# The diagonal tile of inverse softmax sums with its row blocks innermost, and a new order of issue

## The chip, the core and the metric

The kernel runs on one core of a Trainium2 chip. The core has five engines that run side by side, each through its own queue of instructions in order: TensorE (PE in the profile; matmuls, and PEld for the loading of their stationary operand), VectorE (DVE), ScalarE (ACT), GpSimd (POOL) and SyncE (SP), which here only issues transfers to the 16 DMA engines. SBUF is the working memory of 128 partitions, PSUM the memory that TensorE writes. An instruction on one engine that needs a result of another waits for a semaphore; everything behind it on its own queue waits with it. The metric is the time of one execution on the device, in microseconds.

## What is computed

Attention over 4 batches of 12 heads, 448 positions and 64 features, then a gated block with a product over positions, then a layer norm with a feed-forward block of 768 to 3072 to 768 and a residual. Cut to what matters:

```python
def _attn_ref(q, k, v, g_q, g_k):
    q_n, k_n = (rmsnorm(q, g_q), rmsnorm(k, g_k))
    scores = scale * np.matmul(q_n, k_n.transpose(0, 1, 3, 2))
    scores = scores - np.max(scores, axis=-1, keepdims=True)
    attn = np.exp(scores)
    attn = attn / (np.sum(attn, axis=-1, keepdims=True) + 1e-09)
    return np.matmul(attn, v).astype(np.float32)
...
def _moe_ref(x, w_in, w_spatial, b_spatial, w_out):
    h = np.maximum(x @ w_in, 0.0)
    u, v = (h[..., :d_ff // 2], h[..., d_ff // 2:])
    v_n = (v - mu) / np.sqrt(var + 1e-06)
    v_s = np.einsum('ts,bsd->btd', w_spatial, v_n) + b_spatial[None, :, None]
    return ((u * v_s) @ w_out).astype(np.float32)
...
def _moe2_ref(x, g_ln, w_ch1, w_ch2):
    xn = (x - mu) / np.sqrt(var + 1e-06) * g_ln
    ch = np.maximum(xn @ w_ch1, 0.0) @ w_ch2
    return (x + ch).astype(np.float32)
```

## The kernel before

The 48 heads are worked through as 24 pairs (`i` = 0 to 23; six pairs make a batch). A pair occupies the 128 partitions as 2 heads of 64. The 448 positions of a head are cut into 64 x 7: a position is `s = 7 * p + n`, with `p` from 0 to 63 and the row block `n` from 0 to 6 (`NB` = 7). So the queries of row block `n` are positions n, 7 + n, 14 + n and so on.

For each pair, `att_load` brings q, k and v (tiles `raw`, `vraw`); `att_front` and `att_back` normalise q and k (squares `sq`, row sums `ss`, factors `rs`, the product `raw` at L200, a split into two 16-bit halves `qk` at L202 and L203) and transpose them by DMA into `hT` (L206, L208). `s_mm` (L240) makes the scores of one or two row blocks in PSUM (`ps_s`), `softmax1` takes their maxima (`nb`, L251, VectorE) and the exponentials with their sums (`pexp` and `sm`, L256, ScalarE), and `softmax2` transposes the exponentials, on TensorE for the first six pairs (`ps_t`, `pT`) and by DMA for the others (`p`, `pT`). `av_mm` multiplies with v into `ps_o`, which holds the 64 features of both heads on the partitions and the 448 queries along the free dimension, row block by row block: column `64 * n + p`.

The division by the sums comes last. `av_scale` inverts the sums (`sm`, 128 x 7), splits them into two 16-bit parts (`s16`, named `s` in the profile) and multiplies them with a doubled 64 x 64 unit matrix (`eye2`, `eye` in the profile) into a tile `dg` of diagonals (L314, VectorE). Two matmuls with a matrix of ones per head (`head`, L319) spread `dg` over the partitions into `ps_r`; ScalarE copies it to `rb` (L321). `av_out` multiplies `ps_o` with `rb` into `xo` (L332, VectorE), now in the order of the positions, column `7 * p + n`, and splits it into two 16-bit halves `xT`. Both inputs of L332 are read through a rearrangement, `d (n p) -> d p n`, so they step 64 elements from one output element to the next.

Beside the attention of pairs 0 to 6 the weights of the gated block are prepared. Weights come as 64-bit floats, and VectorE makes 32-bit floats of each block in three integer steps (L420 to L422; blocks `v_w`, `u_w`, `o_w`, later `r_w`). The gated block of a batch (`moe1`: `psv`, `psu`, `pss`, `pso`) runs beside the attention of the next batch, that of the last batch beside layer norms and weights of the feed-forward block, which fills the time from 590 us on (`ps1` and `ps`, L729 and L780).

The order of all instructions is set at the end by `issue_order`. It reads the finished program, gives each instruction a cost by rules (`hold`, `LAT`), and lists the engines' work forwards and backwards in turn; the priorities of a pass come from the ends of the one before. A table `SHAKES` of triples (seed, spread, passes) perturbs the priorities at each entry and lists again. The last list becomes the order on every engine, held by dependencies that `add_manual_dep` adds; SP's list, and so the order of the transfers, is one of them. For VectorE the costs depend on sizes, types and memories, not on steps between elements.

Of the kernel before, what the change touches and what calls it, by code (L numbers as in the profile page):

```python
# [10 lines left out]
F16 = mybir.dt.float16  # L11
# [4 lines left out]
ALU = mybir.AluOpType  # L16
# [4 lines left out]
P = 128  # L21
B, H, S, D = 4, 12, 448, 64
NB = 7
# [280 lines left out]
def av_scale(c, i):  # L304

    nc = c.nc
    p = c.pr[i]
    nc.vector.tensor_scalar(p.sm, p.sm, 1e-9, None, op0=ALU.add)
    nc.vector.reciprocal(p.sm, p.sm)
    s16 = c.small.tile([P, 2, NB], F16, tag="s16", name=f"s16_{i}", bufs=2)  # L310
    nc.vector.tensor_scalar(s16[:, 0], p.sm, 2.0 ** 15, None, op0=ALU.mult)
    nc.vector.scalar_tensor_tensor(s16[:, 1], p.sm, 2.0 ** 15, s16[:, 0], op0=ALU.mult, op1=ALU.subtract)
    dg = c.att.tile([P, 2, NB, 64], F16, tag="dg", name=f"dg{i}", bufs=1)
    nc.vector.tensor_tensor(dg.rearrange("p t n q -> p (t n) q"),  # L314
                            s16.rearrange("p t n -> p (t n)").unsqueeze(2).to_broadcast([P, 2 * NB, 64]),
                            c.eye2[:].unsqueeze(1).to_broadcast([P, 2 * NB, 64]), op=ALU.mult)
    pr = c.ps_o.tile([P, 512], F32, tag="ps_o", name=f"ps_r{i}")
    for t in range(2):
        nc.tensor.matmul(pr[:, :S], c.head, dg[:, t].rearrange("p n q -> p (n q)"), start=(t == 0), stop=(t == 1))  # L319
    p.rb = c.att.tile([P, S], F32, tag="rb", name=f"rb{i}", bufs=1)  # L320
    nc.scalar.activation(p.rb, pr[:, :S], AF.Copy, scale=2.0 ** -15 if i in PE_PAIRS else 2.0 ** -29)  # L321


def av_out(c, i):
    nc = c.nc
    p = c.pr[i]
    b, hp = i // NPAIR, i % NPAIR
    if hp == 0:
        c.xT[b] = c.xpools[b % 2].tile([P, NC6, 2, S], F16, tag="xT", name=f"xT{b}")
    xT = c.xT[b]  # L330
    x = c.att.tile([P, S], F32, tag="xo", name=f"xo{i}", bufs=1)
    nc.vector.tensor_tensor(x.rearrange("d (p n) -> d p n", n=NB), p.po[:, :S].rearrange("d (n p) -> d p n", n=NB),  # L332
                            p.rb.rearrange("d (n p) -> d p n", n=NB), op=ALU.mult)
    if i in PE_PAIRS:
        split(c, x, xT[:, hp, 0, :], xT[:, hp, 1, :], c.sv[b][:, 0:1])
    else:
        nc.scalar.activation(xT[:, hp, 0, :], x, AF.Copy)
        nc.vector.tensor_tensor(xT[:, hp, 1, :], x, xT[:, hp, 0, :], op=ALU.subtract)
    del c.pr[i]
# [6 lines left out]
def att_slot(c, i, n):  # L346
# [25 lines left out]
    if i > 0:  # L372
        av_scale(c, i - 1)
        av_mm(c, i - 1)
        yield AV_COST
        av_out(c, i - 1)
# [17 lines left out]
def split(c, raw, hi, lo, scale):  # L394

    c.nc.scalar.activation(hi, raw, AF.Copy, scale=scale)  # L396
    c.nc.vector.scalar_tensor_tensor(lo, raw, scale, hi, op0=ALU.mult, op1=ALU.subtract)
# [399 lines left out]
def weave(a, b):  # L797

    out = [iter(a), iter(b)]
    while out:  # L800
        for g in list(out):
# [10 lines left out]
WINDOW = 3413  # L812


SHAKES = ((0, 0, 2), (556, 3000, 2), (1748, 20000, 1), (1711, 1000, 3), (1453, 8000, 1), (1124, 20000, 1), (257, 300,
# [3 lines left out]


def free_size(ap):
# [225 lines left out]
def issue_order(tc):  # L1047
# [3 lines left out]
    prio = [float(o.n) for o in g.ops]  # L1051
    for seed, spread, passes in SHAKES:
        rnd = random.Random(seed)
# [205 lines left out]
```

## Time and profile before

| what | value |
|---|---|
| median of 3 runs | 1159.89 us (1159.18 to 1160.92) |
| the profiled execution | 1165.11 us on the device |
| its span, first to last instruction | 1163.3 us |
| mean granted clock of TensorE | 0.97 of full speed |
| busy: TensorE, VectorE, ScalarE, GpSimd | 1051.7, 959.1, 587.3, 269.5 us |
| instructions | 16645 |

A busy TensorE means that a matmul is under way, not that it runs at its best rate. Stages are given as stretches of the profiled span, "58:174" from 58 to 174 us. In the rows, names are those of the tiles with their numbers left out, and `a<-b,c` means that a is written from b and c. The DMA share is the mean busy share of the 16 DMA engines; the clock is what TensorE was granted, 1.00 being 2.4 GHz and 0.50 being 1.2 GHz.

### The profile page before, as it was taken

Reading aid. Unit: us, or ns where it says so; the run is one execution under the profiler, and the core shown is the slowest. Engines: PE = TensorE matmul, PEld = TensorE weight load, DVE = VectorE, ACT = ScalarE, POOL = GpSimd, SP = SyncE. Lnnn points to the kernel's source line nnn. Section 1 sums busy time; section 2 is a strip of 40 time slices with the busy share of each in tenths; the row PEclk is TensorE's granted clock in tenths of the full one; section 3 lists DMA queues with packets and bytes.
Section 4 is the critical chain, followed back from the end, with each engine's and each line's share of the span. In section 5 each row is a group of like instructions: output and inputs, shape, how many; then the busy total and the mean of one; then the engine's idle time right before and its main releaser. Section 6 shows DMA issues by size and latency. Waiting matters only on the chain.

```text
span 1163.3 us, 16645 instructions
## 1 busy us (share of the span) xinstructions
PE 1051.7 (90%) x6190; PEld 543.4 (47%) x6190; DVE 959.1 (82%) x1641; ACT 587.3 (50%) x1128; POOL 269.5 (23%) x193
## 2 busy tenths in 40 slices
PE   0689579998889989897699999999999999999998
PEld 0344234444344434443355555555555555555554
DVE  7799999969997996979979788787878878787545
ACT  2899977767776884556532333142432323243110
POOL 3453653418445511222101101010110101011000
PEclk9999879999899999988899999999999999999999
DMA  7997999898999997879572222202121221110004
GB/s 240 233 234 207 189 181 190 160 233 162 205 179 212 182 166 194 183 183 250 127 195 82 82 83 58 78 28 82 34 76 66 74 78 46 65 51 32 1 28 163
DMA packets 249088, 154.46 MB, mean 133 GB/s; under 512 B 209904, under 2 KB 226224, under 8 KB 249008
## 3 DMA queue, kind: packets, MB, share of 16 engines
q1 hardware_dynamic: 244624, 142.40, 51.9%
q10 hardware_dynamic: 4384, 11.01, 3.1%
q8 instruction: 48, 0.79, 0.3%
q14 instruction: 32, 0.26, 0.1%
HBM read 86.40 MB, written 11.01 MB: 84 GB/s over the span
## 4 chain that ended last, share of the span: by engine, by line
PE 45%; DVE 8%; DMA 1%; ACT 1%; issue 1%; POOL 0%; DVEq 0%; ACTq 0%
PE ps L780 24%; PE ps1w L729 6%; PE ps1z L729 6%; PE ps1x L729 6%; PE ps1y L729 3%; DVE x L784 2%; DVE w1v L537 1%; DVE x L694 1%; DMA r_w<-in_moe_w_ch_dram 1%; DVE h L742 1%; DVE lst L681 0%; ACT r_f L525 0%; DVE r_f L422 0%; DVE r_f L421 0%; POOL rsr_x L567 0%
## 5 line engine op out<-in xcount | busy, mean ns | idle before, releaser
L780 PE MATMUL ps<-w,h 128*128 128x384 f16 x2016 | 385.9, 329 | 13.2 <-ACT w L396 5.1
L780 PEld LDWEIGHTS <-h 128*128 128x128 f16 x2016 | 197.2, 98 | 164.4 <-issue 15.1
L784 DVE SCALAR_TENSOR_TENSOR x<-ps,wio,x 128x768 f32<-128x768 f32 x168 | 169.5, 1013 | 75.2 <-PE ps L780 74.3
L729 PEld LDWEIGHTS <-w1v 128*128 128x128 f16 x1512 | 147.0, 98 | 127.4 <-issue 3.7
L240 PE MATMUL ps_s<-hT 128*64 128x448 f16 x672 | 104.4, 392 | 26.1 <-ACT pexp L256 20.3
L256 ACT ACTIVATE pexp<-ps_s,nb 128x448 f32<-128x448 f32 x168 | 106.1, 645 | 25.8 <-DVE nb L251 23.0
L528 POOL TENSOR_TENSOR sums<-r_f 128x384 f32<-128x384 f32 x12 | 12.1, 1011 | 457.7 <-ACT r_f L525 457.7
L729 PE MATMUL ps1x<-xnT,w1v 128*128 128x448 f16 x432 | 108.4, 352 | 0.2 <-DVE tc L736 0.2
L729 PE MATMUL ps1z<-xnT,w1v 128*128 128x448 f16 x432 | 106.3, 352 | 0.0
L729 PE MATMUL ps1w<-xnT,w1v 128*128 128x448 f16 x432 | 105.2, 352 | 1.0 <-DVE tu L736 0.9
L251 DVE TENSOR_REDUCE nb<-ps_s 128x2 f32<-128x896 f32 x96 | 91.8, 964 | 9.4 <-PE ps_s L240 8.9
L240 PEld LDWEIGHTS <-hT 128*64 128x64 f16 x672 | 39.6, 116 | 80.4 <-issue 53.1
L276 DVE SCALAR_TENSOR_TENSOR p<-pexp,p 128x896 f16<-128x896 f32 x72 | 72.7, 1014 | 4.6 <-ACT p L275 4.1
L185 POOL TENSOR_TENSOR rs<-ss,mhalf 128x28 f32<-128x28 f32 (+1 forms) x12 | 60.0, 4997 | 29.1 <-DVE ss L182 20.9
L203 POOL TENSOR_TENSOR qk<-raw,qk 128x896 f16<-128x896 f32 x23 | 46.1, 2005 | 78.7 <-ACT qk L202 67.5
L613 PE MATMUL psu<-xT,w_u 128*128 128x448 f16 x288 | 61.9, 357 | 2.1 <-ACT vr L595 2.0
L591 PE MATMUL psv<-w_v,xT 128*128 128x512 f16 (+1 forms) x360 | 63.5, 339 | 0.1
L275 ACT ACTIVATE p<-pexp 128x896 f16<-128x896 f32 x72 | 61.3, 857 | 2.6 <-DMA pT<-p 2.4
L741 ACT ACTIVATE h<-td 128x448 f16<-128x448 f32 x24 | 13.8, 574 | 93.1 <-DVE td L736 93.1
L650 PE MATMUL pso<-w_o,g 128*128 128x384 f16 x288 | 52.9, 327 | 1.9 <-ACT g L636 1.1
L631 PE MATMUL pss<-w_sp,vn 128*128 128x448 f16 (+1 forms) x176 | 46.7, 381 | 8.8 <-DVE u L635 7.4
L729 PE MATMUL ps1y<-xnT,w1v 128*128 128x448 f16 x216 | 53.0, 352 | 0.9 <-DMA xnT<-x 0.9
(229 smaller groups left out, 1672.3 us busy)
## 6 DMA issues: line engine op xcount, KB each, us to landing
r_w<-in_moe_w_ch_dram SPq DMA_DIRECT2D x48, 768.0 KB, 4.4
raw<-in_q_dram SPq DMA_DIRECT2D x24, 224.0 KB, 3.7
raw<-in_k_dram SPq DMA_DIRECT2D x24, 224.0 KB, 4.4
vpre<-in_v_dram SPq DMA_DIRECT2D x12, 448.0 KB, 4.8
hT<-hT SPq DMA_DIRECT2D x48, 112.0 KB, 3.1
vraw<-in_v_dram SPq DMA_DIRECT2D x24, 224.0 KB, 3.7
lv<-x2d SPq DMA_DIRECT2D x16, 336.0 KB, 4.5
x<-x2d ACTq DMA_DIRECT2D x14, 384.0 KB, 4.2
```

The source lines that it names most:

```text
L185: nc.gpsimd.tensor_tensor(rs, ss, c.mhalf[:, 0:14 * m], op=ALU.pow)
L240: nc.tensor.matmul(ps[hd * 64:hd * 64 + 64, :S], p.hT[:, blk, hd * 64:hd * 64 + 64], kt[:, :, hd * 64:hd * 64 + 64], start=(t == 0), stop= ...
L251: nc.vector.tensor_reduce(nb[:, 0:n], ps[:, 0:n, :S], axis=AX.X, op=ALU.max, negate=True)
L256: nc.scalar.activation(pe[:, j, :], ps[:, j, :S], AF.Exp, bias=nb[:, j:j + 1], scale=1.0, accum_out=p.sm[:, blk:blk + 1])
L275: nc.scalar.activation(p16[:, 0:n, 0], x, AF.Copy, scale=2.0 ** 14)
L276: nc.vector.scalar_tensor_tensor(p16[:, 0:n, 1], x, 2.0 ** 14, p16[:, 0:n, 0], op0=ALU.mult, op1=ALU.subtract)
L591: nc.tensor.matmul(ps[m * h:m * h + m, 0:hn], xT[:, k, x, t * P:t * P + m], wv[:, w, k, h * hn:(h + 1) * hn], start=(n == 0), stop=(n == l ...
L613: nc.tensor.matmul(ps[:, :S], wu[:, w, k, f * P:(f + 1) * P], xT[:, k, x, :], start=(n == 0), stop=(n == len(mms) - 1))
L650: nc.tensor.matmul(ps[:, 0:384], g16[:, f, g, s0:s0 + m], wo[:, w, f, e * 384:(e + 1) * 384], start=(n == 0), stop=(n == len(mms) - 1))
L729: nc.tensor.matmul(ps, w[:, a, x, d], xnT[:, :, 21 * y + 3 * b + d], start=first and n == 0, stop=n == 8, skip_group_check=True)
L780: nc.tensor.matmul(ps[:, e, 0:QK], h16[:, f, x, t * P:(t + 1) * P], w2[:, y, f, e * QK:(e + 1) * QK], start=n == 0, stop=n == 5)
L784: nc.vector.scalar_tensor_tensor(x2, ps[:, :, 0:QK], io[:, 0:1], x2, op0=ALU.mult, op1=ALU.add)
```

## The change

In `av_scale`, `dg` is laid out as `[P, 2, 64, NB]` instead of `[P, 2, NB, 64]`: of its 896 elements per partition the 7 row blocks are now next to each other. Its two inputs are broadcast accordingly, `s16` over the 64 in the middle and `eye2` over the 7 innermost; before, `s16` was broadcast over the innermost 64. The output of L314 is contiguous before and after. `ps_r` and `rb` then stand in the order of the positions, and `av_out` reads `rb` contiguously; `ps_o` is still read with a step of 64. Sizes, types and the number of instructions are the same.

The second part is the table `SHAKES`, 14 entries in place of 23, of which a line each is shown:

```diff
@@ -310,13 +310,12 @@
     s16 = c.small.tile([P, 2, NB], F16, tag="s16", name=f"s16_{i}", bufs=2)
     nc.vector.tensor_scalar(s16[:, 0], p.sm, 2.0 ** 15, None, op0=ALU.mult)
     nc.vector.scalar_tensor_tensor(s16[:, 1], p.sm, 2.0 ** 15, s16[:, 0], op0=ALU.mult, op1=ALU.subtract)
-    dg = c.att.tile([P, 2, NB, 64], F16, tag="dg", name=f"dg{i}", bufs=1)
-    nc.vector.tensor_tensor(dg.rearrange("p t n q -> p (t n) q"),
-                            s16.rearrange("p t n -> p (t n)").unsqueeze(2).to_broadcast([P, 2 * NB, 64]),
-                            c.eye2[:].unsqueeze(1).to_broadcast([P, 2 * NB, 64]), op=ALU.mult)
+    dg = c.att.tile([P, 2, 64, NB], F16, tag="dg", name=f"dg{i}", bufs=1)
+    nc.vector.tensor_tensor(dg, s16[:].unsqueeze(2).to_broadcast([P, 2, 64, NB]),
+                            c.eye2[:].unsqueeze(1).unsqueeze(3).to_broadcast([P, 2, 64, NB]), op=ALU.mult)
     pr = c.ps_o.tile([P, 512], F32, tag="ps_o", name=f"ps_r{i}")
     for t in range(2):
-        nc.tensor.matmul(pr[:, :S], c.head, dg[:, t].rearrange("p n q -> p (n q)"), start=(t == 0), stop=(t == 1))
+        nc.tensor.matmul(pr[:, :S], c.head, dg[:, t].rearrange("p q n -> p (q n)"), start=(t == 0), stop=(t == 1))
     p.rb = c.att.tile([P, S], F32, tag="rb", name=f"rb{i}", bufs=1)
     nc.scalar.activation(p.rb, pr[:, :S], AF.Copy, scale=2.0 ** -15 if i in PE_PAIRS else 2.0 ** -29)
 
@@ -330,7 +329,7 @@
     xT = c.xT[b]
     x = c.att.tile([P, S], F32, tag="xo", name=f"xo{i}", bufs=1)
     nc.vector.tensor_tensor(x.rearrange("d (p n) -> d p n", n=NB), p.po[:, :S].rearrange("d (n p) -> d p n", n=NB),
-                            p.rb.rearrange("d (n p) -> d p n", n=NB), op=ALU.mult)
+                            p.rb.rearrange("d (p n) -> d p n", n=NB), op=ALU.mult)
     if i in PE_PAIRS:
         split(c, x, xT[:, hp, 0, :], xT[:, hp, 1, :], c.sv[b][:, 0:1])
     else:
...
-SHAKES = ((0, 0, 2), (556, 3000, 2), (1748, 20000, 1), (1711, 1000, 3), (1453, 8000, 1), (1124, 20000, 1), (257, 300,
...
+SHAKES = ((0, 0, 5), (1794, 40000, 3), (1412, 40000, 2), (941, 40000, 1), (167, 20000, 3), (1631, 3000, 1), (1820,
...
```

The layout alone leaves the planner's list of every engine as it was; the table changes it on all engines. Up to its 692nd instruction, the last `xo` at 445.2 us in the profile, VectorE's list holds the same instructions before and after, in another order. Lines below `av_scale` have numbers lower by one in the changed kernel, those below the table lower by two.

First place: SP's queue from its first transfer on, before. `raw_111` is q and k of pair 0, `raw_165` and `raw_171` are those of pairs 1 and 2, `gg` and `gk` the two gain vectors, `v_w` the first blocks of the gate's weights.

```order
L160 DMA raw_111<-in_q_dram 128x448
L112 DMA gg<-in_g_q_dram 128x64
L113 DMA gk<-in_g_k_dram 128x64
L1126 DMA gln<-in_moe_g_ln_dram 128x6x1
L468 DMA bp<-in_moe_b_spatial_dram 64x7
L416 DMA v_w_258<-in_moe_w_in_dram 128x1024
L416 DMA v_w_263<-in_moe_w_in_dram 128x1024
L161 DMA raw_111<-in_k_dram 128x448
```

The same rows now:

```order
L415 DMA v_w_258<-in_moe_w_in_dram 128x1024
L112 DMA gg<-in_g_q_dram 128x64
L113 DMA gk<-in_g_k_dram 128x64
L1124 DMA gln<-in_moe_g_ln_dram 128x6x1
L467 DMA bp<-in_moe_b_spatial_dram 64x7
L160 DMA raw_111<-in_q_dram 128x448
L161 DMA raw_111<-in_k_dram 128x448
L160 DMA raw_165<-in_q_dram 128x448
```

The first weight block moved to the front, ahead of `gg` and `gk`; the second left its place between q and k of pair 0 and stands behind these eight.

Second place: VectorE at the first pair's normalisation, before. `rsq` and `rs` are the factors, `raw_111` the product at L200, `qk_0` the 16-bit split, `v_f` the three integer steps of a weight block, `vparts` maxima over v.

```order
L421 SCALAR_TENSOR_TENSOR v_f<-v_w_290,v_f 128x512
L102 TENSOR_TENSOR rsq_q_146<-rs_143 128x14
L422 SCALAR_TENSOR_TENSOR v_f<-v_w_290,v_f 128x512
L145 TENSOR_REDUCE vparts_190<-vpre_0_191 128x1
L103 SCALAR_TENSOR_TENSOR rsq_q_146<-rsq_q_146,ss_137 128x14
L104 SCALAR_TENSOR_TENSOR rs_143<-rsq_q_146,rs_143 128x14
L189 TENSOR_SCALAR rs_143<-rs_143,qa 128x7
L200 TENSOR_TENSOR raw_111<-raw_111,rs_143 128x896
L145 TENSOR_REDUCE vparts_190<-vpre_1_194 128x1
L200 TENSOR_TENSOR raw_165<-raw_165,rs_187 128x896
L203 TENSOR_TENSOR qk_0_158<-raw_111,qk_0_158 128x14x64
```

And now:

```order
L104 SCALAR_TENSOR_TENSOR rs_143<-rsq_q_146,rs_143 128x14
L189 TENSOR_SCALAR rs_143<-rs_143,qa 128x7
L200 TENSOR_TENSOR raw_111<-raw_111,rs_143 128x896
L145 TENSOR_REDUCE vparts_190<-vpre_1_194 128x1
L200 TENSOR_TENSOR raw_165<-raw_165,rs_187 128x896
L203 TENSOR_TENSOR qk_0_158<-raw_111,qk_0_158 128x14x64
L419 TENSOR_SCALAR v_f<-v_w_290 128x512
L200 TENSOR_TENSOR raw_171<-raw_171,rs_187 128x896
L420 SCALAR_TENSOR_TENSOR v_f<-v_w_290,v_f 128x512
L145 TENSOR_REDUCE vparts_190<-vpre_2_197 128x1
L421 SCALAR_TENSOR_TENSOR v_f<-v_w_290,v_f 128x512
```

The three steps of `v_w_290` moved from ahead of the product `raw_111` to behind the split `qk_0`.

Third place: VectorE around the maxima `nb` of pair 6, for which ScalarE and, behind it, TensorE wait; `o_f` are integer steps of a weight block, `wsp` splits of the spatial weights, `p` a split of exponentials. Before:

```order
L420 TENSOR_SCALAR o_f<-o_w_1400 128x768
L421 SCALAR_TENSOR_TENSOR o_f<-o_w_1400,o_f 128x768
L422 SCALAR_TENSOR_TENSOR o_f<-o_w_1400,o_f 128x768
L332 TENSOR_TENSOR xo_1367<-ps_o_1318,rb_1316 128x448
L251 TENSOR_REDUCE nb_1_1279<-ps_s_1_1265 128x2
L251 TENSOR_REDUCE nb_2_1297<-ps_s_2_1288 128x2
```

And now, from the second integer step on:

```order
L420 SCALAR_TENSOR_TENSOR o_f<-o_w_1400,o_f 128x768
L396 SCALAR_TENSOR_TENSOR xT_534<-xo_1194,wsc_V_210,xT_534 128x448
L421 SCALAR_TENSOR_TENSOR o_f<-o_w_1400,o_f 128x768
L487 TENSOR_TENSOR bp<-bp,b_1347 64x7
L180 TENSOR_REDUCE ss_1937<-sq_1938 128x14
L276 SCALAR_TENSOR_TENSOR p_6_0_1284<-pexp_0_1262,p_6_0_1284 128x2x448
L251 TENSOR_REDUCE nb_1_1279<-ps_s_1_1265 128x2
L396 SCALAR_TENSOR_TENSOR wsp_2_1274<-wspraw_1124,wsc_sp,wsp_2_1274 112x448
L396 SCALAR_TENSOR_TENSOR wsp_3_1327<-wspraw_1124,wsc_sp,wsp_3_1327 112x448
L462 COPY wsp_2_1274<-wsp_2_1274 112x2x64
L251 TENSOR_REDUCE nb_2_1297<-ps_s_2_1288 128x2
```

The integer steps are spread out, with `xT`, `ss` and `p` between them and `nb_1`; `nb_2` is three rows behind `nb_1` instead of next to it, and `xo` comes later, behind `nb_2`.

## Rows read from the trace of the kernel before

**Rows 1.** The page's head and its part 1: busy us, share, instructions.

```profile
span 1163.3 us, 16645 instructions
...
PE 1051.7 (90%) x6190; PEld 543.4 (47%) x6190; DVE 959.1 (82%) x1641; ACT 587.3 (50%) x1128; POOL 269.5 (23%) x193
```

**Rows 2.** By stage: us; PE, PEld, DVE, ACT, POOL busy; clock, DMA share, GB/s.

```profile
29.00:58.00 29.00, 20.11 (x118) 10.01 (x119) 21.66 (x50) 23.84 (x54) 12.85 (x7) 1.00 0.92 232
58.00:174.00 116.00, 91.26 (x514) 41.71 (x511) 111.91 (x199) 102.39 (x221) 58.61 (x34) 0.87 0.91 203
174.00:232.00 58.00, 57.02 (x373) 25.72 (x372) 54.68 (x92) 43.57 (x90) 23.45 (x17) 1.00 0.92 177
...
261.00:350.00 89.00, 78.41 (x516) 35.90 (x514) 85.00 (x134) 66.99 (x138) 51.64 (x31) 0.94 0.94 181
350.00:380.00 30.00, 28.39 (x191) 13.76 (x189) 22.59 (x33) 20.04 (x41) 17.83 (x10) 1.00 1.03 207
380.00:445.00 65.00, 58.90 (x393) 26.05 (x389) 59.21 (x103) 49.36 (x106) 17.93 (x13) 1.00 0.95 181
...
590.00:1163.30 573.30, 567.32 (x3272) 318.02 (x3270) 433.47 (x684) 174.55 (x322) 43.79 (x40) 1.00 0.21 70
```

**Rows 3.** Waits, 58 to 445 us: us in total, times, longest us.

```profile
ACT pexp L256 <- DVE nb L251: 20.6, 22, 3.5
...
PE ps_s L240 <- ACT pexp L256: 20.3, 17, 3.8
```

**Rows 4.** Tiles `rb` and `dg`: ns min/median/max, first and last start us.

```profile
L332 DVE TENSOR_TENSOR xo<-ps_o,rb x24: 897/926/964, 63.1 to 445.2; 128x448 f32<-128x448 f32 x24
...
L314 DVE TENSOR_TENSOR dg<-s,eye x24: 1069/1082/2771, 51.9 to 437.9; 128x896 f16<-128x896 f16 x24
```

**Rows 5.** Groups by shape, VectorE: busy us, mean ns; idle us before.

```profile
L736 DVE SCALAR_TENSOR_TENSOR tb<-ps1z,tq 128x448 f32<-128x448 f32 x24 | 14.8, 615 | 1.4 <-PE ps1z L729 1.4
```

**Rows 6.** Line 332 alone by stage: VectorE busy us (instructions), clock, DMA share.

```profile
58.00:174.00 116.00, 6.50 (x7) 0.87 0.91 203
...
261.00:350.00 89.00, 4.59 (x5) 0.94 0.94 181
...
380.00:445.00 65.00, 4.63 (x5) 1.00 0.95 181
```

**Rows 7.** VectorE in order of time from the start: start us, us [idle before].

```profile
6.62 0.22 DVE L114 TENSOR_TENSOR gg<-gg,gk 128x64 f32<-128x64 f32 x1 [4.93 <-DMA gk<-in_g_k_dram]
...
13.16 1.07 DVE L180 TENSOR_REDUCE ss<-sq 128x14 f32<-128x896 f32 x1
...
19.35 0.41 DVE L420 TENSOR_SCALAR v_f<-v_w 128x512 int32<-128x512 int32 x1
...
19.80 0.69 DVE L421 SCALAR_TENSOR_TENSOR v_f<-v_w,v_f 128x512 int32<-128x512 int32 x1
...
20.52 0.69 DVE L422 SCALAR_TENSOR_TENSOR v_f<-v_w,v_f 128x512 int32<-128x512 int32 x1
...
22.85 1.09 DVE L200 TENSOR_TENSOR raw<-raw,rs 128x896 f32<-128x896 f32 x1
...
25.86 1.08 DVE L203 TENSOR_TENSOR qk<-raw,qk 128x896 f16<-128x896 f32 x1
```

**Rows 8.** ScalarE's first square; DMA rate from 0 to 30 us in 40 slices.

```profile
10.40 0.95 ACT L179 ACTIVATE sq<-raw 128x896 f32<-128x896 f32 x1 [8.17 <-DMA raw<-in_q_dram]
...
GB/s 0 0 65 264 23 22 19 14 343 339 371 372 377 406 397 372 277 273 109 311 306 49 16 124 368 373 220 384 328 375 314 203 179 361 380 384 322 156 136 148
```

**Rows 9.** Two stretches, columns as in Rows 2; score matmuls by tile `hT`.

```profile
116.00:145.00 29.00, 16.01 (x99) 7.41 (x98) 28.24 (x55) 26.79 (x58) 18.05 (x12) 0.83 0.91 190
145.00:174.00 29.00, 23.14 (x120) 10.29 (x120) 27.94 (x53) 22.00 (x43) 15.36 (x9) 0.76 0.96 179
...
L240 PE MATMUL ps_s<-hT x672: 349/353/583, 32.9 to 427.3; 128*64 128x448 f16 x168
```

**Rows 10.** VectorE in order of time, an integer step of `o_w_1400`.

```profile
126.72 1.66 DVE L421 SCALAR_TENSOR_TENSOR o_f<-o_w,o_f 128x768 int32<-128x768 int32 x1
```

More of the change, by code (lines that the diff above doesn't have):

```diff
@@ L812 @@
 WINDOW = 3413
-SHAKES = ((0, 0, 2), (556, 3000, 2), (1748, 20000, 1), (1711, 1000, 3), (1453, 8000, 1), (1124, 20000, 1), (257, 300,
[3 rows of a table removed]
+SHAKES = ((0, 0, 5), (1794, 40000, 3), (1412, 40000, 2), (941, 40000, 1), (167, 20000, 3), (1631, 3000, 1), (1820,
+          40000, 1), (767, 300, 1), (482, 1000, 2), (1711, 40000, 1), (573, 300, 1), (1160, 40000, 1), (799, 1000, 1),
+          (523, 20000, 1))
 def free_size(ap):
```

3 rows, old and new, of the table SHAKES are left out of this document.

## The prediction

> **What bounds the kernel now.** I read the busy times first [rows 1]: TensorE 90%, VectorE 82% of the span, so no engine is full throughout. The table by stage [rows 2] tells where each one limits. From 590 us to the end (573.3 us) TensorE is busy 567.3 us at full clock; neither part of the change shortens a matmul there, and the 6.0 idle us include the way out at the end. So the time is decided by how early TensorE reaches this state. The attention part, 58 to 445 us, is of two kinds. In 58:174, 261:350 and 380:445 VectorE is busy 111.9 of 116, 85.0 of 89 and 59.2 of 65 us while TensorE stands idle 24.7, 10.6 and 6.1 us: VectorE is the bound. In 174:232 and 350:380 TensorE is busy 57.0 of 58 and 28.4 of 30 us: there (and between, to 261 us) a faster VectorE buys little. The waits say how VectorE holds TensorE up [rows 3]: the score matmuls `ps_s` wait 20.3 us for the exponentials, and these 20.6 us for the row maxima `nb` on VectorE. The DMA engines' share is 0.91 to 1.03 in all these stretches [rows 2], a third resource with little room.
>
> **The change, part by part.**
>
> *The product `xo` (L332).* It takes 897 to 964 ns, 926 in the middle, 24 times [rows 4]. Its output is contiguous; its two inputs step 64 floats from one element to the next, one in PSUM (`po`), one in SBUF (`rb`). The nearest row of the same size, with one PSUM and one SBUF input and all operands contiguous, is the `tb` group of L736: 615 ns [rows 5]. So the steps cost 311 ns. After the change `rb` is contiguous and `po` still steps. No row has a single stepped operand, so the new cost lies between 615 ns (all the penalty was `rb`'s) and 926 ns (`po` alone sets it). I take the lower end, 0.62 us. The argument, not a row, is that TensorE writes a PSUM column every 0.8 ns (353 ns for 448 columns [rows 9]), faster than VectorE reads one (615 / 448 = 1.4 ns), so that PSUM should be the memory with room for a step; the other end is the first rival. The saving is 24 x 0.311 = 7.5 us of VectorE. Where it lies is counted by stage [rows 6]: 7 of the 24 in 58:174 and 5 in 261:350, where TensorE idles most: 12 x 0.311 = 3.7 us, counted in full. 5 lie in 380:445, and one starts at 445.2 [rows 4, 6], where VectorE is 91% busy and the DMA share 0.95: 6 x 0.311 = 1.9 us, counted by half, 0.9. The other 6 lie where TensorE is full and hides them: nothing now; without that cover they would bring 1.9 us more. Sum: 4.6 us.
>
> One rule speaks against it. The Trainium skill, Vector Engine (DVE) Microarchitecture Reference, section 5.2 Measured stream behaviour on trn2, gives 1.73 ns per column when one source hops at every element and 1.76 when both do. It was measured in SBUF; if a PSUM input counted alike, an estimate from that page takes 448 x 0.03 = 13 ns off each `xo` and 0.3 us off VectorE in all, where the sum above takes 7.5. No run here shows yet which holds.
>
> *The diagonal `dg` (L314).* 1069 ns at the least, 1082 in the middle, for 896 elements [rows 4]. Before, one input repeats each of its elements 64 times; after, the other repeats each of its elements 7 times and the first runs in rows of 7 halves. Output, types and count are the same. The `qk` subtraction, 896 contiguous elements, takes 1.08 us too [rows 7], so `dg` pays no penalty today that a new layout could lift: a gain is excluded, and I take no change. Upper bound: each element pays what a stepped element of `xo` pays, 311 / 448 = 0.69 ns, 896 x 0.69 = 0.62 us more (third rival). The matmuls `ps_r`, the copy to `rb` and the output of `xo` have the same sizes and contiguous operands on both sides: nothing.
>
> *The order, at the start.* VectorE works almost without a pause up to the first pair's `raw` product at 22.85 us [rows 7]. Before, the three integer steps of the weight block `v_w_290` (0.41, 0.69 and 0.69 us [rows 7]) stand ahead of it; after, behind the `qk` subtraction that follows (second place in the change). So `raw`, the transposes that wait for `qk`, and the first scores can come 1.79 us sooner. Upper end: the row sums `ss` at 13.16 us wait today for VectorE and not for `sq`, which ends at 10.40 + 0.95 us [rows 7, 8]; 1.8 us more if VectorE is freed there too. Lower end: a 512 KB weight block now stands ahead of `gk` on SP's queue (first place), and VectorE waits 4.93 us for `gk` [rows 7]. If `gk` lands later by the 1.5 us that 512 KB take at some 350 GB/s [rows 8], the gain is gone. The three steps have to be done later all the same; VectorE has idle time for them just behind, as 29:58 holds 21.7 us of VectorE work [rows 2]. I let 1.0 us reach the end, with 0 and 3.6 as bounds.
>
> *The order elsewhere.* The new order moves most rows, but mostly by a few places. The third place is typical: there TensorE waits for the maxima of pair 6. The integer steps of `o_w_1400` (one of them 1.66 us [rows 10]) no longer stand in one block ahead of `nb_1`, but the sums `ss` and the split `p` now do, and `nb_2`, which followed `nb_1` at once, has two `wsp` splits ahead of it. One maximum gains, the next loses. Up to the last `xo` VectorE has the same instructions in both orders, and no stage as a whole is brought forward. No sign follows: I take 0, with a bound of 4 us either way, about a third of the 13.9 us that VectorE idles in the three stretches that it bounds (4.1, 4.0 and 5.8 [rows 2]).
>
> **Sum.** The profiled execution took 1165.1 us with a span of 1163.3, 5.2 above the median of the runs, 1159.9. 1165.1 - 4.6 - 1.0 = 1159.5 for an execution like the profiled one; the same 5.6 us off the median give **1154.3 us**. Late next are, in 58:174, the DMA engines (share 0.91), and in 380:445 TensorE.
>
> **The rivals.**
>
> *First: `po` alone sets `xo`.* The layout change then does nothing for the time, the product stays near 0.92 us, and only the start is left: 1159.9 - 1.0 = 1158.9 us. For it: `po` steps as far as `rb` did, and one slow stream is enough to slow a product. Against it stands only the argument on PSUM. The page's rule quoted above, read for PSUM, is this case.
>
> *Second, slower: the order brings another stretch at half clock.* In 116:145 TensorE is busy only 16.0 of 29 us at a mean granted clock of 0.83, and in 145:174 the clock is 0.76 [rows 9]: behind the pauses it stood at the lower level, 1.2 GHz, for about (0.17 + 0.24) x 29 / 0.5 = 24 us, where a score matmul takes up to 583 ns instead of 353. In 261:350 TensorE is near this state, 78.4 of 89 us and 0.94 [rows 2]. If the new order adds one such stretch there, TensorE loses 24 x (1 - 353 / 583) = 9.5 us, and the five `xo` there (1.6 us) save nothing: 1154.3 + 9.5 + 1.6 = 1165.4 us. It decides the sign from (5.6 - 1.6) / 0.39 = 10 us of added time at half clock on. For it: the places of the pauses change with the order. Against: the third place shows as much gained as lost.
>
> *Third, slower: `dg` pays for its rows of 7.* 24 x 0.62 = 15 us of VectorE, of which as large a part reaches the end as of `xo`, 4.6 / 7.5: 9.1 us, 1154.3 + 9.1 = 1163.4 us. It eats the gain of `xo` from 0.31 us on each `dg`.
>
> *Fourth: the order gains its 4 us elsewhere and the start its 3.6:* 1154.3 - 4 - 2.6 = 1147.7 us.
>
> **How the numbers follow.** Chances: forecast 0.42, first rival 0.30, second 0.18, third 0.06, fourth 0.04. Some 0.2% (2.3 us) is what a measurement of this kernel can tell from no change. Around each case stand the order's 4 us. Faster by over 0.2% (under 1157.6): 0.83 of the forecast, 0.37 of the first rival, a tenth of the third, all of the fourth, 0.35 + 0.11 + 0.01 + 0.04 = 0.51. Slower (over 1162.2): 0.02, 0.11, 0.75 and 0.6 of the first four cases, 0.01 + 0.03 + 0.13 + 0.04 = 0.21. The rest, 0.28, is no change. The range runs from the forecast less the bounds of the order, the start and the six hidden `xo`, 1154.3 - 4 - 2.6 - 1.9 = 1145.8, to 1164, which leaves out over half of the second rival and some of the third.
>
> **What would show it.** `xo` near 0.62 us: the layout step is right; near 0.92: the first rival. `dg` off 1.08 us: the third. The first score matmul, at 32.9 us now [rows 9], should start by 31 to 32 us. With the forecast right, TensorE's idle time in 58:174 and 261:350 falls by about 4 us together, and the stretch behind 590 us is the old one moved forward by some 5 us. A clock below 0.94 in 261:350 speaks for the second rival. The prediction is wrong if the saving appears as idle time of VectorE, or if the order alone moves any stretch by more than 4 us.

## The result: slower, 1.0103 of the time before

The changed kernel takes 1173.51 us (median of 4 runs, 1170.27 to 1174.88), the kernel before 1160.41 us beside it (4 runs, 1159.18 to 1164.35). The ratio is 1.0103, 95% interval 1.0069 to 1.0137. Forecast were 1154.3 us with a range of 1145.8 to 1164.0: the sign was wrong, and the time lies 9.5 us outside the range. The profiled execution took 1174.74 us with a span of 1172.9.

The page of the changed kernel, head and part 1 (busy us, share, instructions), beside [rows 1]:

```profile
span 1172.9 us, 16660 instructions
...
PE 1048.9 (89%) x6190; PEld 546.5 (47%) x6190; DVE 958.4 (82%) x1641; ACT 586.3 (50%) x1128; POOL 286.8 (24%) x193
```

The two products, by tile: ns least/median/most, first and last start in us. They answer [rows 4]:

```profile
L331 DVE TENSOR_TENSOR xo<-ps_o,rb x24: 570/615/625, 66.5 to 450.8; 128x448 f32<-128x448 f32 x24
...
L314 DVE TENSOR_TENSOR dg<-s,eye x24: 1045/1084/1102, 48.7 to 441.8; 128x896 f16<-128x896 f16 x24
```

`xo` fell from 926 to 615 ns, the 615 ns of the contiguous `tb` [rows 5]; `dg` is where it was (1082 before). So the layout did what was forecast, and the kernel is slower all the same.

By stage (us; PE, PEld, DVE, ACT, POOL busy; TensorE's granted clock as a share of 2.4 GHz; DMA share; GB/s), to be laid beside [rows 2] and [rows 9]:

```profile
29.00:58.00 29.00, 21.60 (x117) 10.87 (x117) 24.74 (x51) 24.65 (x54) 13.57 (x7) 1.00 1.02 252
58.00:174.00 116.00, 84.15 (x470) 39.57 (x470) 106.78 (x186) 97.81 (x212) 63.67 (x30) 0.83 0.83 194
174.00:232.00 58.00, 57.52 (x378) 25.62 (x378) 51.81 (x89) 41.59 (x81) 25.54 (x19) 1.00 0.94 188
261.00:350.00 89.00, 81.06 (x550) 37.86 (x548) 78.91 (x128) 66.90 (x141) 44.57 (x27) 0.98 0.96 184
350.00:380.00 30.00, 22.88 (x120) 9.67 (x120) 24.50 (x34) 18.37 (x37) 17.55 (x11) 0.89 0.95 201
380.00:445.00 65.00, 61.56 (x428) 27.82 (x426) 60.52 (x103) 51.17 (x113) 17.97 (x13) 1.00 0.89 164
...
116.00:145.00 29.00, 17.10 (x93) 7.62 (x91) 24.83 (x48) 23.58 (x49) 21.15 (x10) 0.74 0.80 181
145.00:174.00 29.00, 17.56 (x86) 7.48 (x85) 27.53 (x46) 20.31 (x42) 14.98 (x8) 0.62 0.88 179
...
515.00:590.00 75.00, 54.24 (x261) 26.94 (x260) 67.44 (x136) 38.63 (x55) 15.80 (x12) 0.87 0.89 196
```

TensorE's busy time and the number of its matmuls (in brackets) tell where the time went. In 29:58 it was busy 1.5 us longer than before (21.60 against 20.11), though with no more matmuls (117 against 118), in 261:350 2.7 us longer with 34 more. But in 58:174 it was busy 7.1 us less (84.15 against 91.26, 470 matmuls against 514), most of it in 145:174 (17.56 against 23.14), and there its clock was lower too: 0.62 means that for 0.38 x 29 / 0.5 = 22 of the 29 us the granted clock was 1.2 GHz, against 14 us before (0.76). In 350:380 it was busy 5.5 us less, and the clock is 0.89 instead of 1.00. VectorE, which was to be relieved, idles 9.2 us in 58:174 instead of 4.1.

### The profile page after: what moved, and what is told of

It reads as the page before. It is cut to its first block, busy times and chain, and to the rows that moved or that the text cites. A ratio compares the mean times of both kernels' runs of the same rounds, so it can differ in the third digit from the quotient of the medians.

```text
span 1172.9 us, 16660 instructions
## 1 busy us (share of the span) xinstructions
PE 1048.9 (89%) x6190; PEld 546.5 (47%) x6190; DVE 958.4 (82%) x1641; ACT 586.3 (50%) x1128; POOL 286.8 (24%) x193
## 4 chain that ended last, share of the span: by engine, by line
PE 48%; DVE 7%; DMA 1%; issue 0%; POOL 0%; ACT 0%; DVEq 0%
PE ps L779 26%; PE ps1w L728 6%; PE ps1z L728 6%; PE ps1x L728 6%; PE ps1y L728 3%; DVE x L783 1%; DVE w1v L536 1%; DVE x L693 1%; DMA xnT<-x 1%; DVE h L741 1%; DVE r_f L420 0%; DVE lst L680 0%; DVE r_f L421 0%; POOL rsr_x L566 0%; DVE w L396 0%
## 5 line engine op out<-in xcount | busy, mean ns | idle before, releaser
L779 PE MATMUL ps<-w,h 128*128 128x384 f16 x2016 | 380.1, 331 | 17.3 <-ACT h L740 5.9
L783 DVE SCALAR_TENSOR_TENSOR x<-ps,wio,x 128x768 f32<-128x768 f32 x168 | 168.4, 1013 | 74.8 <-PE ps L779 74.1
L240 PE MATMUL ps_s<-hT 128*64 128x448 f16 x672 | 100.9, 389 | 27.2 <-ACT pexp L256 22.9
L527 POOL TENSOR_TENSOR sums<-r_f 128x384 f32<-128x384 f32 x12 | 14.7, 1221 | 447.5 <-ACT r_f L524 415.4
L728 PE MATMUL ps1x<-xnT,w1v 128*128 128x448 f16 x432 | 104.7, 352 | 0.7 <-DVE tc L735 0.7
L728 PE MATMUL ps1z<-xnT,w1v 128*128 128x448 f16 x432 | 103.6, 352 | 0.0
L728 PE MATMUL ps1w<-xnT,w1v 128*128 128x448 f16 x432 | 100.8, 352 | 0.0
L612 PE MATMUL psu<-xT,w_u 128*128 128x448 f16 x288 | 59.1, 353 | 0.9 <-ACT vr L594 0.8
L748 ACT ACTIVATE tp<-ps1x 128x448 f32<-128x448 f32 x24 | 13.0, 543 | 85.9 <-PE ps1x L728 85.8
```

Source lines behind the costliest of these rows:

```text
L240: nc.tensor.matmul(ps[hd * 64:hd * 64 + 64, :S], p.hT[:, blk, hd * 64:hd * 64 + 64], kt[:, :, hd * 64:hd * 64 + 64], start=(t == 0), stop= ...
L612: nc.tensor.matmul(ps[:, :S], wu[:, w, k, f * P:(f + 1) * P], xT[:, k, x, :], start=(n == 0), stop=(n == len(mms) - 1))
L728: nc.tensor.matmul(ps, w[:, a, x, d], xnT[:, :, 21 * y + 3 * b + d], start=first and n == 0, stop=n == 8, skip_group_check=True)
L779: nc.tensor.matmul(ps[:, e, 0:QK], h16[:, f, x, t * P:(t + 1) * P], w2[:, y, f, e * QK:(e + 1) * QK], start=n == 0, stop=n == 5)
L783: nc.vector.scalar_tensor_tensor(x2, ps[:, :, 0:QK], io[:, 0:1], x2, op0=ALU.mult, op1=ALU.add)
```

## Experiments

### The two halves of the change apart

The layout alone is the changed kernel with the old table of numbers; every engine then has the order of the kernel before, and the two traces show the same sequence on each.

```diff
-SHAKES = ((0, 0, 5), (1794, 40000, 3), (1412, 40000, 2), (941, 40000, 1), (167, 20000, 3), (1631, 3000, 1), (1820,
...
+SHAKES = ((0, 0, 2), (556, 3000, 2), (1748, 20000, 1), (1711, 1000, 3), (1453, 8000, 1), (1124, 20000, 1), (257, 300,
...
```

> The new layout with the order of before. Theory A (the order lost the time): xo takes 0.62 us as in the changed kernel, and the order of every engine is that of before, so the sum of the prediction holds without its order terms: 4 to 6 us under before, 1154 to 1156 us. Theory B (the layout itself loses, because the shorter xo lets the engines run ahead into buffers, transfers or a half-clock stretch that they then wait for): 1160 us or more, with xo at 0.62 us all the same.

Measured: ratio 0.9969 (0.9953 to 0.9985), 1158.8 us beside 1161.75: 3.6 us faster. A second measurement, beside other kernels:

> The new layout with the order of before, a second time, beside the three others on one chip. By the first measurement (0.31% under before) 1156 to 1160 us; by the sum of the prediction without its order terms, 4.6 us under before.

Measured: 0.9975 (0.9959 to 0.9991), 2.9 us faster. Both medians, 1158.8 and 1159.6 us, lie between the two theories, nearer to B's 1160 than to A's 1156. But the sign is A's: the layout by itself loses nothing, it is a gain of some 3 us, of the 4.6 that the sum gave. The order alone is the kernel before with the new table:

```diff
-SHAKES = ((0, 0, 2), (556, 3000, 2), (1748, 20000, 1), (1711, 1000, 3), (1453, 8000, 1), (1124, 20000, 1), (257, 300,
...
+SHAKES = ((0, 0, 5), (1794, 40000, 3), (1412, 40000, 2), (941, 40000, 1), (167, 20000, 3), (1631, 3000, 1), (1820,
...
```

> The new order with the old layout (xo back at 0.92 us). Theory A: the order's loss, some 18 us, stands alone: 1175 to 1180 us, above the changed kernel by the 4 to 6 us that the layout is worth. Theory B: the order is harmless, 1158 to 1163 us. If it comes out at 1173 us, like the changed kernel, the 7.5 us of VectorE are hidden behind other waits in the new order.

Measured: 1.0116 (1.0085 to 1.0148), 1174.95 us, 13.5 us slower, at the lower edge of theory A. So the order lost the time: 13.5 us by itself, and 1.0103 less some 0.997, 15 us, on top of the layout. Whether `xo` gains anything within the new order (1.0116 against 1.0103) lies inside the intervals.

The layout alone, first its `xo`, then the stretches that answer those of the changed kernel above:

```profile
L331 DVE TENSOR_TENSOR xo<-ps_o,rb x24: 573/613/625, 62.1 to 440.1; 128x448 f32<-128x448 f32 x24
```

```profile
116.00:145.00 29.00, 15.26 (x87) 6.60 (x87) 28.09 (x49) 26.22 (x56) 17.82 (x13) 0.73 0.94 195
145.00:174.00 29.00, 25.58 (x164) 13.21 (x164) 28.20 (x55) 20.94 (x40) 15.75 (x10) 0.86 1.00 187
...
261.00:350.00 89.00, 76.13 (x510) 35.44 (x507) 82.68 (x132) 65.97 (x136) 48.98 (x30) 0.96 0.95 183
350.00:380.00 30.00, 28.47 (x195) 13.21 (x195) 23.30 (x31) 20.26 (x39) 20.87 (x13) 1.00 1.07 202
...
515.00:590.00 75.00, 59.03 (x303) 30.35 (x302) 68.13 (x135) 38.34 (x52) 11.15 (x12) 0.89 0.78 180
```

The order alone (its `xo` is back at 929 ns in the middle):

```profile
145.00:174.00 29.00, 18.93 (x95) 8.08 (x95) 28.06 (x48) 20.30 (x41) 14.88 (x6) 0.65 0.90 182
...
515.00:590.00 75.00, 52.47 (x237) 25.21 (x236) 62.74 (x126) 37.21 (x52) 15.83 (x12) 0.83 0.83 183
```

Two stretches carry the mark of the new order, with either layout. In 145:174 TensorE is busy 17.6 and 18.9 us instead of 25.6, at a clock of 0.62 and 0.65 instead of 0.86. In 515:590, where the first expert's products meet the layernorm of the second half, it is busy 54.2 and 52.5 instead of 59.0. The first mark is the plainer one: of all kernels run here, the six with the old order from the start to 174 us have 23.1 to 26.1 us in 145:174, the seven with the new order 15.7 to 18.9. In 350:380 TensorE is down too, 22.9 and 23.7 us instead of 28.5, but there it had done more before: 550 and 556 matmuls in 261:350 instead of 510.

### Cutting the order in two

Does the loss lie ahead of the last `xo` (445 us) or behind? Two kernels take one table up to a cut and the other behind it. The first list of each engine holds what the planner issues, by one table, ahead of the first write of a named tile; the rest follows in the order of the other.

```diff
+CUT = "xo23"
...
-    for l in schedule(g, prio)[1].values():
+    for e, l in order.items():
+        l = [o for o in l if o.n in early] + [o for o in later[e] if o.n not in early]
         for a, b in zip(l, l[1:]):
```

> New layout; the new order for all that the planner has issued by the first instruction of the last xo (about 445 us), the order of before for the rest. The start times of the two traces put some 8 to 10 us of the new order's loss ahead of this point (the last xo starts 5.6 us later although 7.5 us of VectorE work are gone) and some 8 us behind it (the second third of w1v, 520 to 575 us). Theory A1 (two separate losses): 1162 to 1166 us. Theory A2 (all of it is made ahead of the cut and only shows later): 1171 to 1175 us. Theory A3 (the early delay is taken up behind the cut by the reserve there): 1154 to 1157 us.

Measured: 1.0026 (1.0004 to 1.0047), 1165.1 us, 6 us over the layout alone.

> New layout; the order of before up to the last xo, the new order for the rest. Theory A1 (two separate losses): 1161 to 1165 us. Theory A2 (the loss is made ahead of the cut): 1154 to 1157 us. Theory A3 (all of the loss is made behind the cut): 1171 to 1175 us.

Measured: 1.0040 (1.0020 to 1.0061), 1165.9 us, 8 us over it and 0.9 above A1's range. 6 and 8 make 14 of the 15 us of the whole order, as theory A1 has it: two losses, one on each side. The traces say the same without the sum. The last `xo`, first in the kernel with the new order up to the cut, then in the one with the new order behind it, and TensorE in 515:590 in the latter:

```profile
L331 DVE TENSOR_TENSOR xo<-ps_o,rb x24: 565/614/625, 66.8 to 444.9; 128x448 f32<-128x448 f32 x24
```

```profile
L331 DVE TENSOR_TENSOR xo<-ps_o,rb x24: 575/613/626, 62.1 to 437.0; 128x448 f32<-128x448 f32 x24
```

```profile
515.00:590.00 75.00, 55.97 (x269) 27.95 (x268) 69.16 (x134) 37.58 (x51) 15.87 (x12) 0.83 0.80 175
```

With the new layout and the old order up to it, it starts at 437.0 to 440.1 us in the traces; with the new order, at 444.9 here, at 450.8 in the changed kernel and at 446.9 to 449.5 in three kernels below that move a few instructions. From there to the end of the span it is 716.6 us in the layout alone and 727.1 with the new order behind. The 444.9 and 450.8 belong to the same order of issue: two single traces can differ by 6 us, and smaller differences between them tell little.

### What TensorE waits for, and what comes of moving it

In 143:175, the waits of TensorE (us in total, times, longest) in the layout alone and in the changed kernel:

```profile
PE ps_s L240 <- ACT pexp L256: 1.7, 1, 1.7
PE ps_r L318 <- DVE dg L314: 1.5, 1, 1.5
```

```profile
PE ps_s L240 <- ACT pexp L256: 9.1, 3, 4.2
PE ps_r L318 <- DVE dg L314: 5.3, 1, 5.3
```

The head sums `ps_r` of pair 6 wait for `dg`, and the scores `ps_s` for `pexp`, which in part waits for the maxima on VectorE. Behind 515 us it looks alike. VectorE, then GpSimd, in the kernel with the new order behind the cut (start us, us):

```profile
539.04 1.29 DVE L741 SCALAR_TENSOR_TENSOR h<-tb,h 128x448 f16<-128x448 f32 x1
540.26 1.35 DVE L536 TENSOR_TENSOR w1v<-r_f,w1v 128x384 f16<-128x384 f32 x1
541.53 2.14 DVE L693 TENSOR_TENSOR x<-lv,x 112x1152 f16<-112x1152 f32 x1
543.60 0.55 DVE L536 TENSOR_TENSOR w1v<-r_f,w1v 128x384 f16<-128x384 f32 x1
544.07 1.34 DVE L701 TENSOR_TENSOR lv<-lv 112x384 f32<-112x384 f32 x1
545.33 1.00 DVE L783 SCALAR_TENSOR_TENSOR x<-ps,wio,x 128x768 f32<-128x768 f32 x1
```

```profile
539.94 1.25 POOL L528 TENSOR_TENSOR sums<-sums,r_f 128x384 f32<-128x384 f32 x1
541.16 1.30 POOL L529 TENSOR_TENSOR sums<-r_f 128x384 f32<-128x384 f32 x1
542.42 2.57 POOL L530 TENSOR_TENSOR sums<-r_f,sums 128x384 f32<-128x384 f32 x1
```

And TensorE there:

```profile
546.39 6.39 PE L779 MATMUL ps<-w,h 128*128 128x384 f16 x24 [4.43 <-DVE x L783]
```

The first eviction of `ps` into `x2` (L783) stands behind work for the second expert and the layernorm, and TensorE waits 4.43 us for it. Some of that work is stretched while GpSimd runs: one `w1v` takes 1.35 us where the next takes 0.55, and beside that next one GpSimd's last sum takes 2.57. Against the same rows in the layout alone, `h`, the first `w1v`, `x` and `lv` take some 3 us more together. In the layout alone the first sum meets an eviction, which reads PSUM, and both run at full pace:

```profile
538.11 1.01 DVE L783 SCALAR_TENSOR_TENSOR x<-ps,wio,x 128x768 f32<-128x768 f32 x1
```

```profile
538.40 1.01 POOL L527 TENSOR_TENSOR sums<-r_f 128x384 f32<-128x384 f32 x1 [1.80 <-ACT r_f L524]
```

The Trainium skill, SBUF — State Buffer, section Who interferes with whom, says that a VectorE instruction with two SBUF inputs contends with a GpSimd instruction that reads SBUF, and that one with at most one SBUF input, outside VectorE's 2-port perf modes, does not. The rows above agree, as far as rows that overlap can show it: where VectorE's instruction has two SBUF inputs, now its row is the stretched one, now GpSimd's.

If the place in VectorE's queue makes the loss, moving the awaited instruction up should win it back. Each entry of the edit names a tile and which of its writes is moved, and the tile and write ahead of which it is put, counted from 0; all else stays. Behind the cut, with the old order ahead of it:

```diff
+MOVES = (('h16_0_0', 1, 'x16_1_0_3_1', 0), ('h16_0_0', 2, 'x16_1_0_3_1', 0), ('h16_0_0', 3, 'x16_1_0_3_1', 0), ('x2_0', 0, 'w1v1', 0), ('x2_1', 0, 'w1v1', 1), )
```

> The kernel with the new order behind the last xo, and five VectorE instructions of it moved up, nothing else: the three remaining h of expert 0 (ta, tc, tb) ahead of the 1.74 us x of the layernorm, and the first two evictions of ps into x2 ahead of the first and the second w1v. Theory A (VectorE's queue: these five stand behind 8.5 us of work for expert 1 and for the second half's layernorm, part of it stretched beside GpSimd, and TensorE, with both ps buffers full, waits 4.4 us for the first eviction and 2.1 us for h, and then runs at half clock): 5 to 8 us of the 8 us are won back, 1157 to 1161 us, TensorE's wait for the first eviction is gone, and the half-clock stretch near 536 to 550 us is shorter. Theory B (the work of the new order is simply later everywhere, in transfers, GpSimd or ScalarE): 1164 to 1167 us, and TensorE waits for something else.

Measured: 1.0031 (1.0013 to 1.0050), 1165.0 us, against 1.0040 without the moves: not 5 to 8 us, but 1 us, which the intervals don't tell from nothing. It is theory B. TensorE in that kernel:

```profile
539.36 6.85 PE L779 MATMUL ps<-w,h 128*128 128x384 f16 x24 [3.44 <-DVE x L783]
...
552.49 0.32 PE L779 MATMUL ps<-w,h 128*128 128x384 f16 x1 [1.68 <-DVE rst_x L564]
```

The wait came 7 us sooner but is still 3.4 us long, and a new one follows it. Theory A falls as a price for these five. Ahead of the cut, one instruction:

```diff
+MOVES = (('xo17', 0, 'p16_18_2', 0), )
```

> The kernel with the new order up to the last xo, and one VectorE instruction of it moved up: xo of pair 17 ahead of the third p of pair 18 (2.02 us in the trace) and of the sum of squares behind it (1.07 us). TensorE waits for this xo for 3.2 us with the head sums, and 5 us with the products of the next stage, at half clock. Theory A (again VectorE's queue): 2 to 4 us of the 6.6 us are won back, 1161 to 1163 us against 1165 us. Theory B (xo isn't what the stage waits for, the transfers of the next pairs are): within 1 us of 1165 us.

Measured: 1.0021 (0.9997 to 1.0044), 1164.7 us, against 1.0026: nothing that can be told, theory B. TensorE's wait for this `xo` fell from 3.2 to 1.3 us, and it waited the more for others. Both sets in the changed kernel:

> The changed kernel as it is, with the six VectorE instructions of the two kernels before moved up. Theory A: 8 to 11 us less than the changed kernel, 1162 to 1166 us. Theory B: 1171 to 1175 us.

Measured: 1.0089 (1.0055 to 1.0124) against 1.0103. Theory B, within the intervals. Last, nine instructions of 143 to 167 us in the kernel with the new order up to the cut, with the engine's name ahead:

```diff
+MOVES = (('DVE', 'o3_f', 1, 'p16_6_2', 0), ('DVE', 'o3_f', 2, 'p16_6_2', 0), ('Activation', 'w_o', 3, 'pexp7_2', 0), ('DVE', 's16_6', 0, 'nb7_2', 0), ('DVE', 's16_6', 1, 'nb7_2', 0), ('DVE', 'dg6', 0, 'nb7_2', 0), ('DVE', 'ssb_o', 0, 'sm7', 0), ('DVE', 'nb8_0', 0, 'w_o', 2), ('DVE', 'nb8_1', 0, 'w_o', 2), )
```

> The kernel with the new order up to the last xo (1165 us), and nine instructions of its stretch from 143 to 167 us moved up, eight on VectorE and one on ScalarE: the last clean-up of the w_o weights (o_f) ahead of three p, its maximum on ScalarE ahead of the third pexp of pair 7, the scales and dg of pair 6 ahead of the third maximum of pair 7, and the first two maxima of pair 8 ahead of the last two w_o. TensorE's queue holds the head sums of pair 6 and the four column sums of w_o ahead of all products of the next stage, and waits 5.9 us there, and 2.6 us for the maxima behind w_o. Adding up TensorE's idle time and what half clock takes, the new order is 7 to 13 us behind the layout alone at 174 us, and hardly any further at 445 us. Theory A (these waits in VectorE's queue make the early loss): 4 to 6 us are won back, 1158 to 1161 us, and the stretch from 145 to 174 us loses 3 to 6 us less. Theory B (like the six instructions moved before, the time won is waited for behind): 1163 to 1167 us.

Measured: 1.0023 (1.0004 to 1.0041), 1165.9 us, as without: theory B again. TensorE in the kernel without these moves, then in the one with them:

```profile
153.21 0.53 PE L318 MATMUL ps_r<-dg,head 128*128 128x448 f16 x1 [5.94 <-DVE dg L314]
```

```profile
150.32 0.53 PE L318 MATMUL ps_r<-dg,head 128*128 128x448 f16 x1 [1.17 <-DVE dg L314]
152.53 0.25 PE L83 MATMUL pssc_o<-ssb_o,ones 128*128 128x1 bf16 x4 [1.67 <-DVE ssb_o L80]
...
156.05 0.16 PE L83 MATMUL pssc_V<-ssb_V,ones 128*128 128x1 bf16 x1 [2.89 <-DVE sst_o L85]
```

The wait for `dg` fell from 5.9 to 1.2 us, and the column sums behind it in TensorE's queue now wait 1.7 and 2.9 us: the sum is nearly the same. That suggests that what is late is not one instruction but VectorE's work for this place as a whole; no run shows it by itself.

### Cutting at other places

To find the place ahead of 445 us, the new order was kept up to a tile and the old one put behind it, as one line of parts (table, tile that ends it):

```diff
+PARTS = ((NEW, 'nb17_0'), (OLD, None),)
```

> New layout; the new order up to the first maximum of pair 17 (about 325 us), the order of before from there on. In the traces the new order is 8 to 12 us late at 137 to 255 us and 1 to 6 us early at 272 to 313 us against the layout alone. Theory A (the early part costs nothing net, the loss ahead of the last xo is made at 340 to 366 us): 1155 to 1159 us, perhaps under the layout alone. Theory C (the half-clock stretch at 133 to 168 us costs for good): 1162 to 1166 us.

Measured: 1.0047 (1.0026 to 1.0067), 1167.2 us, above both theories. In 350:380 TensorE is back at 28.95 us at full clock, so that stretch isn't what costs. The same with `'nb6_0'` and with `'nb9_0'`:

> New layout; the new order up to the first maximum of pair 6 (about 126 us), the order of before from there. Theory A (the early loss is made by the order between 126 and 185 us): 1156 to 1160 us, as the layout alone. Theory B (it is made before, by what the first 126 us leave undone): 1163 to 1167 us.

Measured: 1.0027 (1.0009 to 1.0045), 1164.5 us, theory B.

> New layout; the new order up to the first maximum of pair 9 (about 184 us), the order of before from there. Theory A and theory B: 1163 to 1168 us, like the cut at pair 17, for both place the early loss before 185 us. Theory C (it is the 340 to 366 us stretch after all, as TensorE has spent there what could have filled its waits): 1156 to 1160 us.

Measured: 1.0079 (1.0051 to 1.0107), 1172.5 us, above all three theories. With `'nb3_0'`, 78 us of the new order, which is the start that the prediction priced:

> New layout; the new order up to the first maximum of pair 3 (about 78 us), the order of before from there. It measures the prediction's term for the start alone: 1 us under the layout alone, 1157 to 1159 us, if the start is what the prediction took it for. If the start leaves work undone that is paid for in the stretch from 145 to 174 us, as the cut at pair 6 seems to: 1162 to 1166 us.

Measured: 1.0043 (1.0022 to 1.0063), 1166.5 us: the start is not what the prediction took it for, and the loss is 0.5 us above the other case. And the middle part alone:

```diff
+PARTS = ((OLD, 'nb6_0'), (NEW, 'xo23'), (OLD, None),)
```

> New layout; the order of before up to the first maximum of pair 6 (about 120 us), the new order from there to the last xo, the order of before behind it. Theory A (the order from 126 to 185 us makes a loss of its own): 1162 to 1167 us, with over 10 us of TensorE's time lost from 145 to 174 us. Theory B (the loss there is what the first 126 us left undone): 1156 to 1161 us, with some 6 us lost in that stretch, as in the layout alone.

Measured: 1.0014 (0.9996 to 1.0032), 1162.5 us, 4.5 us over the layout alone, at the lower end of theory A. Behind 445 us, `(OLD, 'w1v1'), (NEW, None)`:

> New layout; the order of before up to the first write of w1v for expert 1 on VectorE (about 545 us), the new order from there to the end. Theory A (the late loss is made at 515 to 560 us, where the work of expert 1 and of the second half's layernorm stands ahead of the evictions of expert 0): 1157 to 1160 us, as the layout alone. Theory B (it is made behind, in the 590 us in which TensorE is busy throughout): 1163 to 1168 us.

Measured: 1.0011 (0.9995 to 1.0028), 1162.8 us, 4 to 5 us over the layout alone: between its two theories.

These do not locate the loss. Cuts at 78, 126, 184, 325 and 445 us cost 8, 6, 12, 9 and 6 us against the layout alone, each to some 2 us: no rise, so they are not parts of one sum. The first 126 us (6) and what follows to 445 us (4.5 to 5) make 11, where both together cost 6, barely more than the noise of the four runs. A cut order is a third order and may pay for its seam; no run shows that price alone, and the cut at 445 us is not free of it either. In the stretch itself the new order does show, wherever it stands there; the middle part alone, with the old order up to 120 us:

```profile
145.00:174.00 29.00, 20.21 (x117) 8.64 (x117) 27.86 (x53) 21.14 (x39) 17.64 (x9) 0.79 0.92 183
```

```profile
PE ps_r L318 <- DVE dg L314: 5.9, 1, 5.9
```

TensorE is busy 20.2 us instead of 25.6, and waits for `dg` as long as in the new order. But the kernel with the new order up to pair 3, which has the old order there, is down as well, at 21.6 us:

```profile
145.00:174.00 29.00, 21.60 (x113) 9.88 (x112) 27.78 (x51) 21.78 (x44) 14.72 (x8) 0.73 0.96 186
```

So neither theory on this stretch is enough: its own order costs there, and a kernel that is new only ahead of it is down too, by what it left undone or because it is late and has other work in this window. What all runs have in common is simpler: 13 kernels with the new layout and another order than the old one were run, and all 13 are slower than the layout alone, by 4 to 15 us, their intervals above both of its intervals. They are not 13 orders found apart: all are the one new order, whole, mixed with the old one, or with a few instructions moved. The layout alone is the fastest, and the one that beats both kernels.

## Why the prediction was wrong

**`xo`, right.** 0.62 us at each place, at the lower end that was taken; first rival (the PSUM operand alone sets the pace) refuted. VectorE's `xo` time in 58:174 fell from 6.50 us [rows 6] to 4.25. Of the 4.6 us counted for the end, 2.9 and 3.6 were measured with the order held fixed.

**`dg`, right.** 1084 ns; the third rival falls.

**The start: right at its place, wrong at the end.** The first score matmul moved from 32.9 to 30.1 us, more than forecast:

```profile
L240 PE MATMUL ps_s<-hT x672: 349/353/583, 30.1 to 434.3; 128*64 128x448 f16 x168
```

By 58 us the lead is gone. The score matmuls alone (line 240; busy us and number of TensorE first) in 29:58, before, then in the changed kernel:

```profile
29.00:58.00 29.00, 10.32 (x58) 3.38 (x60) 1.00 0.92 232
```

```profile
29.00:58.00 29.00, 11.24 (x56) 4.17 (x56) 1.00 1.02 252
```

They are 56 instead of 58 (64 in the layout alone), and the first `xo` starts at 66.5 us, where it was 63.1 [rows 4]. And the kernel with only the first 78 us of the new order is 8 us slower than the layout alone, not 1 us faster. The lower bound of 0 was no bound: the step that failed here is that a sooner first score was let through to the end. That the work it left undone is asked for later is the likely reason; the price of the seam is not taken out.

**The order elsewhere: the step that failed.** It was taken as 0 with 4 us either way. Together with the start it measured 15 us of loss on top of the layout, almost four times the bound of 4. Three things in it were wrong. The third place, pair 6, was called typical because one maximum gains and the next loses there; the loss stood 20 us behind it, in 145:174, and behind 515 us, which no place of the prediction touched at all. The bound was worked out from VectorE's 13.9 idle us, but what was lost is TensorE's: 8.0 us more idle than in the layout alone in 145:174, 4.8 in 515:590 (3.1 where only the order behind 445 us is new and nothing ahead of it is late), and time at half clock on top. And gains and losses were taken as equally likely, for which no row spoke; this order lost, whole and in every part that was run.

**Second rival: the right kind, the wrong place.** It had a new stretch at half clock in 261:350. There the clock rose, from 0.94 to 0.98; it fell in 145:174 (0.76 to 0.62) and in 350:380 (1.00 to 0.89). Its 1165.4 us were too few: it had one such stretch, and priced the half clock without the idle time around it.

The two signs named for a wrong prediction were both seen: VectorE's idle time rose (4.1 to 9.2 us in 58:174, more than the 2.25 us saved there), and the order moved a stretch by more than 4 us.

**What stays open.** Shown: the layout gains, the order loses, on both sides of 445 us, with TensorE starved in the same two stretches under either layout. Not shown: what in the order makes it. The waits for single instructions of VectorE's queue are real, but moving these up passed the wait on. The stretching beside GpSimd is seen in rows, and was not tried by itself. The table changes the lists of all engines at once, the transfers among them, and no run changed the list of one engine alone; in 143:175 none of TensorE's waits ends with a DMA, in either kernel, so there the transfers are not what TensorE waits for directly.

## What to carry to other kernels

A new order of issue is a change of its own, and its risk can be larger than the edit beside it (here 15 us of loss against 3 us of gain): measure the edit with the order held, and the order with the edit undone. Don't centre the error of a new order on zero because one place gains and the next loses; here a first score that came 2.8 us sooner had lost its lead 28 us later. And the instruction that an engine waits for is only the first in its queue: look at what the next ones need before moving it up.

## What the runs showed of the hardware

VectorE reads a PSUM operand that steps 256 bytes from one element to the next as fast as a contiguous one: 615 ns for 448 columns with only `po` stepping, 615 ns for `tb`, another operation of the same size, with nothing stepping, 926 ns when `rb` in SBUF stepped too. The Trainium skill, Vector Engine (DVE) Microarchitecture Reference, section 5.2 Measured stream behaviour on trn2, gives 1.73 ns per column where one source hops at every element and 1.054 where all is contiguous. Worked out from these, an estimate for one hop is 0.68 ns per column, 303 ns for 448 columns. The hop of `rb` in SBUF cost 926 - 615 = 311 ns, which agrees; that of `po` in PSUM cost nothing, so the price doesn't carry over to a PSUM source.

An instruction with two SBUF inputs was stretched beside GpSimd from 0.55 to 1.35 us, and an eviction from PSUM beside the same kind of GpSimd work not at all (1.01 us). Which of the two stands there is the order's doing.
